# Gated recurrence and causal-convolution kernel: the gate tangents issued per chunk and per gate, the first three chunks in one root batch, a new written order

## The chip, the cores and the metric

The kernel runs on one core of a Trainium2 chip. The metric is the device time of one execution in microseconds (us). Three executions of the kernel before took 302.71, 301.36 and 300.97 us; the median is 301.36 us.

The engines are named as the profile names them: PE (TensorE, matmuls and transposes), PEld (its weight loads), DVE (VectorE), ACT (ScalarE), POOL (GpSimd) and SP (SyncE, which here only issues the DMAs). Each engine works off its own queue in order; an instruction that waits holds everything behind it on that engine.

## The reference, cut to what matters

The input x and two gate inputs have the shape 4 x 6336 x 256 in fp32. With c = 8 and a per-channel constant a_base:

```python
sig_r = 1/(1+exp(-r_gate));  sig_i = 1/(1+exp(-i_gate))
a_t   = exp(c * sig_r * log(a_base))
norm  = sqrt(max(1 - a_t*a_t, 1e-6))
h_t   = a_t * h_{t-1} + norm * sig_i * x          # scan over time, per batch row
# second stage, on y = h
gate  = sigmoid(causal 5-tap depthwise convolution of y)
out   = (gate * (y @ w_val)) @ w_out
```

Both sigmoids of the first stage are computed as tanh of half the argument: sig = (1 + tanh(x/2))/2. So every element of r_gate and i_gate passes once through a tanh on ACT, every a_t through an exp on ACT, and every 1 - a² through a square root on ACT.

## The kernel before, in words

The 25,344 time steps (4 x 6336) are cut into 51 **windows**: windows 0, 1 and 50 of 256 steps, all others of 512. A window is loaded with 128 partitions, each holding consecutive steps of all 256 channels. Windows are bound into 28 **chunks**: chunks 0, 1 and 2 are windows 0, 1 and 2; chunks 3 to 25 hold two windows each (chunk c holds windows 2c - 3 and 2c - 2); chunks 26 and 27 are windows 49 and 50. After the transposes the two halves of 128 channels, h = 0 and 1, lie on the partitions.

There are no loops in time: the whole program is one string, ORDER, of words such as `th.5` or `tr.3.1@0,1` (operation, window or chunk, half, and the banks of the accumulator memory PSUM behind the @). The words are emitted in turn, each on its engine, so ORDER is the order of every engine's queue and also of SP's queue of DMAs. The words:

| word | engine | what it does |
|---|---|---|
| lr, li, lx (window) | SP | loads of r, i and x, 512 KB for a 512-step window |
| th (window) | ACT | tanh of r and i of one window together, 2048 elements per partition (L289) |
| pp, up (window) | POOL | tanh of i plus one (L297), then times x into uring (L309) |
| xp, uv (window) | PE, DVE | the same product for six windows by way of PSUM (L314, L323) |
| tr, ex (chunk group, half) | PE, ACT | transpose of tanh r (L334), exp of it into aring (L350); GROUPS binds one or two chunks |
| sq, sa (chunk, half) | POOL, ACT | a² into ering (L358, L366) |
| rt (batch) | ACT | the root over a batch of chunks (L377); BATCHES binds the chunks |
| nt, xg, xt, sc (chunk) | PE, DVE, PE, DVE | transpose the roots back (L392), multiply into uring (L399), transpose (L408), scan (L430) |
| cv, tg (window) | PE, ACT | convolution in 20 matmuls (L442), tanh of the gate (L449) |
| vl, gv, ou (window) | PE, DVE, PE | y @ w_val (L457), times the gate (L462), times w_out (L472) |
| cd or ca, st (window) | DVE or ACT, SP | copy of the result from PSUM (L480 or L482), store |

The root needs another function table of ACT than tanh and exp. Where a word of the other kind comes next, the loop at the end of the kernel issues a table load (L509); there are 20 of them in the kernel before, besides two at the start.

The data around the tangents lie in rings. `riring` (L201) holds r and i of four windows; r and i of a window are freed together by its `th`. `tring` (L203) holds the tangents of three windows in three lanes each: the tangent of i always lies in the middle lane, that of r in the first lane in one round of three windows and in the last lane in the next (`swapped`, L263), so that the next tangent of r need not wait for the transposes of the last one. The lane of i is freed by `up` or `uv`. `xring` holds x of four windows, freed by `up` or `xp`. `oring` holds four windows of output, freed by the stores. A load waits on SP until its slot is free, and every DMA behind it waits too.

Of the kernel before, what the change touches and what calls it, by code (L numbers as in the profile page):

```python
# [18 lines left out]
BATCHES = [[0], [1], [2], [3, 4], [5, 6, 7], [8, 9, 10], [11, 12, 13], [14, 15, 16], [17, 18, 19], [20, 21, 22], [23, 24,  # L19
    25], [26, 27]]  # L20
# [6 lines left out]
NTRI = 3  # L27
# [11 lines left out]
s_wl.2 lr.8 li.10 lx.8 xt.2@2,3 xt.1@0,1 sc.1.1 li.9 lr.10 sq.3.0 rt.3 li.11 up.6 sc.1.0 lx.10 lr.11 sc.2.1 sc.2.0
up.5 th.8 lx.11 s_wcast th.10 lx.9 pp.10 up.10 lr.14 th.9 li.13 li.14 lr.13 xp.8@4,5 li.12 lr.12 uv.8 th.11 li.15  # L40
nt.3@0,1 xg.3 nt.4@6,7 pp.11 up.11 cv.1@2,3 tg.1 xg.4 xt.3@0,1 sc.3.1 vl.1@4,5 tr.5.0@6,7 ex.5.0 sq.5.0 tr.5.1@2,3
gv.1 ou.1.0@1 cd.1.0 st.1 lx.12 lr.15 ex.5.1 vl.0@4,5 xp.9@6,7 th.14 sq.5.1 cv.2@2,3 sc.3.0 th.13 uv.9 lx.13 xt.4@1,0
gv.0 ou.0.0@4 cd.0.0 st.0 sc.4.1 lx.15 cv.3@6,7 th.12 li.16 li.18 tr.7.1@4,5 tg.2 vl.2@2,3 gv.2 tg.3 ex.7.1 sq.6.1
sq.6.0 lx.14 pp.14 pp.12 up.12 tr.7.0@6,7 ex.7.0 sq.7.0 lx.16 cv.4@2,3 tg.4 th.15 ou.2.0@4,5 cd.2.0 sc.4.0 st.2 lr.18
lr.16 vl.3@6,7 xp.13@2,3 vl.4@4,5 gv.4 sq.7.1 rt.4 uv.13 th.16 sq.8.1 sq.8.0 pp.15 up.15 li.17 lr.17 up.14 ou.4.0@4,5
li.19 cv.5@0,1 lr.19 gv.3 cd.4.0 lx.17 tg.5 ou.3.0@6,7 lx.18 st.4 cd.3.0 st.3 nt.5@4,5 li.20 xg.5 pp.16 up.16 th.17
pp.17 lr.20 nt.7@6,7 xg.7 lx.19 li.21 nt.6@2,3 xg.6 th.18 pp.18 lr.21 xt.5@4,5 sc.5.1 up.17 vl.5@6,7 cv.6@0,1 tg.6
th.19 tr.9.1@2,3 ex.9.1 li.22 lr.22 up.18 sq.9.1 pp.19 gv.5 sc.5.0 tr.9.0@6,7 ex.9.0 lx.20 ou.5.0@0,1 cd.5.0 sq.10.1
xt.6@5,4 up.19 sc.6.1 cv.7@0,1 tg.7 cv.8@2,3 th.20 lr.24 tg.8 sc.6.0 vl.6@6,7 gv.6 xt.7@0,1 cv.9@4,5 ou.6.0@6,7 sc.7.0
th.21 tg.9 cd.6.0 vl.7@2,3 gv.7 vl.9@6,7 th.22 tr.11.0@0 sc.7.1 ou.7.0@2,3 vl.8@4,5 sq.9.0 tr.12.0@1 gv.9 ou.9.0@6,7  # L50
gv.8 ou.8.0@4,5 sq.10.0 st.5 cd.7.0 cd.9.0 lx.22 st.6 rt.5 lx.21 nt.8@6,7 lr.23 li.23 cd.8.0 nt.9@4,5 pp.22 pp.21
up.22 pp.20 up.20 up.21 xg.8 ex.12.0 xg.9 ex.11.0 li.24 st.7 st.9 li.25 lr.25 lx.23 lx.24 li.26 lr.26 th.23 xt.8@6,7
sc.8.0 sq.11.0 pp.23 sq.12.0 lr.27 li.27 cv.11@2,3 tg.11 cv.10@4,5 sc.8.1 cv.12@0,1 st.8 th.24 pp.24 tg.10 tg.12
vl.11@2,3 tr.11.1@6 ex.11.1 gv.11 vl.10@4,5 gv.10 th.25 xt.9@0,1 sc.9.0 tr.12.1@2 ex.12.1 ou.11.0@6,7 cd.11.0
ou.10.0@4,5 cd.10.0 cv.14@2,3 up.23 lx.25 lx.27 th.26 nt.10@6,7 sc.9.1 st.11 li.29 st.10 tg.14 tr.13.0@4,5 xg.10 up.24
sq.11.1 th.27 ex.13.0 tr.13.1@2,3 vl.12@0,1 gv.12 sq.12.1 li.30 lr.30 lx.26 pp.25 pp.27 sq.13.0 xt.10@6,7 sc.10.1
ex.13.1 sq.13.1 up.27 sq.14.0 pp.26 up.25 lr.28 cv.13@4,5 tg.13 vl.13@0,1 gv.13 li.28 vl.14@2,3 gv.14 ou.12.0@4,5
cd.12.0 ou.13.0@0,1 cd.13.0 ou.14.0@2,3 cv.15@4,5 lr.29 st.13 lx.28 lr.31 sc.10.0 cv.16@0,1 cd.14.0 rt.6 nt.11@6,7
tg.15 tg.16 xg.11 vl.15@2,3 gv.15 th.28 st.12 li.31 lx.29 sq.14.1 up.26 nt.13@4,5 xg.13 pp.28 up.28 nt.12@0,1 xg.12
li.32 vl.16@2,3 gv.16 lx.31 lr.32 lx.30 xt.11@4,5 sc.11.1 sc.11.0 ou.15.0@6,7 th.30 pp.30 th.29 pp.29 cv.18@0,1  # L60
ca.15.0 lr.34 li.34 up.29 cv.17@2,3 tg.18 xt.12@6,7 tg.17 vl.17@0,1 gv.17 tr.15.1@2,3 tr.15.0@4,5 th.31 sc.12.0
ou.17.0@0,1 cd.17.0 sc.12.1 ex.15.1 ex.15.0 cv.20@2,3 tg.20 li.33 lr.33 ou.16.0@0,1 cd.16.0 th.32 vl.18@4,5 gv.18
pp.31 up.31 th.34 xt.13@2,3 sc.13.1 vl.19@6,7 cv.19@0,1 tg.19 gv.19 st.17 st.14 st.16 st.15 up.30 th.33 sq.16.1 lx.32
sc.13.0 li.35 lr.35 lx.33 ou.18.0@4,5 cd.18.0 lx.34 li.36 sq.15.0 lr.38 cv.21@0,1 sq.15.1 vl.21@6,7 st.18 lx.35 lr.36
tg.21 gv.21 vl.20@0,1 sq.16.0 cv.22@2,3 gv.20 li.38 lr.37 li.37 pp.34 ou.19.0@4,5 cd.19.0 pp.33 pp.32 up.32
ou.21.0@6,7 ou.20.0@0,1 rt.7 cd.21.0 st.21 tg.22 cd.20.0 nt.14@4,5 xg.14 st.19 nt.16@6,7 xg.16 vl.22@0,1 gv.22 th.35
up.33 up.34 pp.35 tr.17.1@2,3 ex.17.1 xt.14@4,5 sc.14.0 sc.14.1 tr.17.0@6,7 ex.17.0 cv.23@0,1 cv.24@2,3 tg.23 tg.24
ou.22.0@6,7 cd.22.0 nt.15@0,1 xg.15 vl.24@2,3 vl.23@4,5 gv.23 st.20 st.22 lx.36 gv.24 up.35 cv.26@6,7 sq.17.1 th.36
pp.36 sq.18.0 th.38 xt.15@0,1 sc.15.0 sc.15.1 th.37 pp.37 sq.18.1 sq.17.0 ou.23.0@4,5 tg.26 ca.23.0 cv.25@2,3 tg.25
tr.19.0@6,7 ex.19.0 sq.19.0 xt.16@4,5 sc.16.0 tr.19.1@2,3 ex.19.1 sc.16.1 cv.27@0,1 ou.24.0@6,7 cd.24.0 tg.27  # L70
vl.25@2,3 vl.26@0,1 sq.19.1 rt.8 cv.28@4,5 gv.26 up.36 sq.20.1 li.39 st.23 lx.38 lr.40 pp.38 gv.25 lx.37 vl.27@6,7
gv.27 ou.26.0@0,1 cd.26.0 ou.25.0@2,3 lr.41 lr.39 tg.28 th.39 st.24 cd.25.0 ou.27.0@6,7 cd.27.0 nt.19@0,1 nt.17@2,3
xg.17 xg.19 cv.29@6,7 tg.29 sq.20.0 up.37 up.38 nt.18@4,5 xg.18 vl.28@2,3 gv.28 vl.29@6,7 gv.29 xt.17@0,1 sc.17.1
li.40 th.40 tr.21.1@4 li.41 th.41 pp.40 pp.39 st.26 st.25 tr.21.0@5 ex.21.1 ex.21.0 lx.39 li.42 ou.29.0@6,7 ca.29.0
lr.42 sc.17.0 st.27 lx.40 xt.18@2,3 up.39 th.42 ou.28.0@4,5 cv.30@6,7 cd.28.0 tg.30 tr.22.1@0 ex.22.1 tr.22.0@1
# [24 lines left out]
def kernel(  # L100
# [82 lines left out]
    with tc.manual_schedule():  # L183
# [79 lines left out]
        def swapped(w):  # L263

            return (w // NTRI) % 2

        def load(w, which):
            n = wins[w]
            J = n // P
            if which == "x":  # L270
                dst = xring[:, w % NX, 0:J, :]
            else:
                dst = riring[:, w % NRI, "ri".index(which) ^ swapped(w), 0:J, :]
# [267 lines left out]
```

## Time and profile before

| | |
|---|---|
| median of three executions | 301.36 us |
| the profiled execution | 300.32 us, of it 298.5 us span from the first to the last instruction |
| ACT busy | 278.8 us (93%), 197 instructions |
| DVE busy | 247.6 us (83%), 206 instructions |
| PE busy | 246.4 us (83%), 2509 matmuls and transposes |
| POOL busy | 232.8 us (78%), 155 instructions |
| DMA | 104.75 MB, of it 78.39 MB read and 25.95 MB written |

The busy time is the union of an engine's instructions. On ACT consecutive instructions overlap by about 0.1 us, so the sum of single durations is a little more. A row of the timeline gives the start, the duration, and in brackets the idle time before it with what ended it; a row with "x2" stands for two neighbouring instructions of one kind. A row of the groups gives the count, the busy sum and the mean duration in ns. A row by stretches gives the busy time of each engine inside the stretch, the granted clock of PE, the share of the 16 DMA engines' time that was busy, and GB/s.

### The profile page before, as it was taken

How to read it: one execution, taken by the hardware profiler on the slowest of the kernel's cores; microseconds unless marked ns; L12 is line 12 of the kernel's file. 1: busy time of each engine (PE TensorE's matmuls, PEld its weight loads, DVE VectorE, ACT ScalarE, POOL GpSimd, SP SyncE). 2: the span in 40 equal slices, each digit the busy share in tenths (PEclk: the TensorE clock that was granted, in tenths of full speed). 3: DMA queues.
4: the chain of work that ended last, by engine and by line, in shares of the span. 5: the costliest groups of instructions: out<-in, count | busy, mean ns of one | idle time of the engine just before them, and what ended most of it. 6: DMA issues, size and time to landing. Idle time of an engine off the chain costs nothing.

```text
span 298.5 us, 6286 instructions
## 1 busy us (share of the span) xinstructions
PE 246.4 (83%) x2509; PEld 167.8 (56%) x2509; DVE 247.6 (83%) x206; ACT 278.8 (93%) x197; POOL 232.8 (78%) x155
## 2 busy tenths in 40 slices
PE   0374577897888598989898899998979999899993
PEld 0134255454556466757664758567647675666662
DVE  2030288849999889999999999999999899899993
ACT  6799999999999999999999999999999999969863
POOL 1478958989999899899999879998995996255300
PEclk9997599999999979999999999999999999999999
DMA  6999999999999999999999998999999977726046
GB/s 252 408 408 385 379 411 407 406 414 406 337 379 370 419 416 415 411 406 321 417 411 375 388 417 335 396 353 361 349 409 419 408 278 270 273 116 248 29 186 246
DMA packets 29995, 104.75 MB, mean 351 GB/s; under 512 B 3335, under 2 KB 3854, under 8 KB 29966
## 3 DMA queue, kind: packets, MB, share of 16 engines
q1 hardware_dynamic: 29952, 104.35, 90.5%
q8 instruction: 19, 0.31, 0.4%
q14 instruction: 10, 0.08, 0.1%
q10 hardware_dynamic: 14, 0.01, 0.0%
HBM read 78.39 MB, written 25.95 MB: 350 GB/s over the span
## 4 chain that ended last, share of the span: by engine, by line
ACT 31%; PE 23%; DVE 13%; issue 13%; DMA 12%; POOL 5%; SPq 1%; ACTq 0%; DVEq 0%; POOLq 0%
ACT tring L289 10%; ACT aring L350 8%; DMA riring<-in_r_gate_dram 7%; DVE yring L430 7%; PE banks L442 5%; ACT tgring L449 5%; PE banks L457 5%; ACT ering L377 4%; PE banks L472 4%; PE banks L392 3%; DMA riring<-in_i_gate_dram 3%; DVE tgring L462 3%; DVE oring L480 2%; DMA xring<-in_x_dram 2%; ACT L509 2%
## 5 line engine op out<-in xcount | busy, mean ns | idle before, releaser
L430 DVE TENSOR_TENSOR_SCAN yring<-aring,yring,banks 128x1024 bf16<-128x1024 f32 (+5 forms) x54 | 106.2, 1988 | 0.9 <-PE banks L408 0.6
L358 POOL TENSOR_TENSOR ering<-aring 128x1024 f32<-128x1024 f32 (+2 forms) x54 | 91.5, 1713 | 9.7 <-ACT aring L350 9.7
L309 POOL TENSOR_TENSOR uring<-tring,xring 128x1024 bf16<-128x1024 bf16 (+1 forms) x45 | 94.6, 2113 | 4.9 <-DMA xring<-in_x_dram 3.5
L289 ACT ACTIVATE tring<-riring 128x2048 bf16<-128x2048 f32 (+1 forms) x51 | 93.8, 1867 | 4.1 <-DMA riring<-in_i_gate_dram 1.9
L297 POOL TENSOR_SCALAR tring<-tring 128x1024 bf16<-128x1024 bf16 (+1 forms) x45 | 45.8, 1026 | 30.5 <-ACT tring L289 30.4
L442 PE MATMUL banks<-yring,diag 64*64 64x512 bf16 (+7 forms) x1080 | 61.9, 361 | 4.6 <-ACT aring L350 1.6
L462 DVE SCALAR_TENSOR_TENSOR tgring<-tgring,banks 128x1024 bf16<-128x1024 bf16 (+1 forms) x51 | 58.9, 1178 | 5.5 <-PE banks L457 4.4
L472 PE MATMUL banks<-wo,tgring 128*128 128x256 bf16 x396 | 51.4, 274 | 4.7 <-DVE tgring L462 3.5
L350 ACT ACTIVATE aring<-banks,khf 128x2048 f32<-128x2048 bf16 (+3 forms) x38 | 54.1, 1474 | 0.5 <-PE banks L334 0.4
L449 ACT ACTIVATE tgring<-banks 128x1024 bf16<-128x1024 f32 (+1 forms) x51 | 50.4, 1009 | 3.4 <-PE banks L442 3.3
L457 PE MATMUL banks<-yring,wv 128*128 128x512 bf16 (+4 forms) x216 | 49.4, 361 | 5.0 <-DVE oring L480 2.2
L472 PEld LDWEIGHTS <-tgring 128*128 128x128 bf16 x396 | 41.0, 114 | 15.7 <-DVE tgring L462 9.6
L442 PEld LDWEIGHTS <-diag 64*64 64x64 bf16 x1080 | 30.3, 106 | 28.8 <-issue 13.6
L377 ACT ACTIVATE ering<-ering 128x4096 bf16<-128x4096 f32 (+5 forms) x15 | 44.9, 3019 | 0.1
L399 DVE TENSOR_TENSOR uring<-banks,uring 128x2048 bf16<-128x2048 bf16 (+2 forms) x28 | 29.8, 1095 | 18.2 <-PE banks L392 17.9
L480 DVE COPY oring<-banks 128x1024 f32<-128x1024 f32 (+1 forms) x35 | 40.6, 1181 | 4.8 <-ACT aring L350 2.4
L334 PE MATMUL banks<-ident_b,tring 128*128 128x128 bf16 x396 | 29.0, 227 | 12.2 <-ACT tring L289 10.4
L334 PEld LDWEIGHTS <-tring 128*128 128x128 bf16 x396 | 25.1, 101 | 17.7 <-ACT tring L289 11.7
L457 PEld LDWEIGHTS <-wv 128*128 128x128 bf16 x216 | 19.7, 97 | 26.3 <-issue 12.4
L392 PE MATMUL banks<-ident,ering 128*128 128x128 f32 x198 | 28.8, 296 | 6.8 <-DVE oring L480 2.6
L392 PEld LDWEIGHTS banks<-ident,ering 128*128 128x128 f32 x198 | 25.9, 208 | 13.5 <-ACT ering L377 7.7
L408 PE MATMUL banks<-ident,uring 128*128 128x128 f32 x198 | 27.5, 282 | 2.6 <-DVE uring L399 2.5
(36 smaller groups left out, 113.1 us busy)
## 6 DMA issues: line engine op xcount, KB each, us to landing
riring<-in_i_gate_dram SPq DMA_DIRECT2D x48, 512.0 KB, 8.2
riring<-in_r_gate_dram SPq DMA_DIRECT2D x48, 512.0 KB, 8.3
xring<-in_x_dram SPq DMA_DIRECT2D x48, 512.0 KB, 8.0
out_dram<-oring SPq DMA_DIRECT2D x48, 512.0 KB, 5.7
riring<-in_r_gate_dram SPq DMA_DIRECT2D x3, 256.0 KB, 6.3
riring<-in_i_gate_dram SPq DMA_DIRECT2D x3, 256.0 KB, 6.5
xring<-in_x_dram SPq DMA_DIRECT2D x3, 256.0 KB, 5.3
out_dram<-oring SPq DMA_DIRECT2D x3, 256.0 KB, 7.3
```

What stands on the lines that cost most here:

```text
L289: nc.scalar.activation(out=tring[:, w % NTRI, a:a + 2, 0:J, :], in_=riring[:, w % NRI, :, 0:J, :], func=ACT.Tanh, scale=0.5)
L309: nc.gpsimd.tensor_tensor(out=u, in0=t1, in1=xt, op=ALU.mult)
L350: nc.scalar.activation(out=dst, in_=src, func=ACT.Exp, scale=khf[:, h:h + 1], bias=khf[:, h:h + 1])
L358: nc.gpsimd.tensor_tensor(out=e, in0=a, in1=a, op=ALU.mult)
L377: nc.scalar.activation(out=ering[:].bitcast(BF16)[:, 4 * o:4 * o + 2 * n], in_=ering[:, 2 * o:2 * o + 2 * n], func=ACT.Sqrt, scale=-0.25, ...
L392: nc.tensor.transpose(out=bank[:, k:k + P], in_=ering[:, e + q:e + wins[w] // 2:nq], identity=ident[:])
L430: nc.vector.tensor_tensor_scan(out=yring[:, h, col:col + o1 - o0], data0=aring[:, h, a_at[c] + o0:a_at[c] + o1], data1=xT[:, o0:o1], initi ...
L442: nc.tensor.matmul(out=gp[oh * 64:oh * 64 + 64, h, a:b], lhsT=diag[half * 64:half * 64 + 64, h, k, :], rhs=yring[half * 64:half * 64 + 64, ...
L449: nc.scalar.activation(out=tgring[:, w % NTG, :, 0:wins[w]], in_=live.pop(("gp", w))[:, :, 0:wins[w]], func=ACT.Tanh, scale=0.5)
L457: nc.tensor.matmul(out=val[:, m, a:b], lhsT=wv[:, hk, m * P:(m + 1) * P], rhs=yring[:, hk, col:col + b - a], start=(hk == 0), stop=(hk == ...
L462: nc.vector.scalar_tensor_tensor(out=tgring[:, w % NTG, :, 0:wins[w]], in0=tgring[:, w % NTG, :, 0:wins[w]], scalar=1.0, in1=live.pop(("va ...
L472: nc.tensor.matmul(out=ops[:, j * D:(j + 1) * D], lhsT=gv[:, hk, j:wins[w]:J], rhs=wo[:, hk, :], start=(hk == 0), stop=(hk == H - 1))
```

## The change

`th` is replaced by two words that work on a chunk and not on a window: `ta` takes the tanh of r, `tb` the tanh of i. For a two-window chunk each is one instruction over 2 x 1024 elements; for the single-window chunks over 1024 or 512. The rings are parted: `rring` and `iring` have four windows each, `taring` six windows of tangents of r, `tbring` four windows of tangents of i. The place of window w in a ring of n is (w + 1) mod n, so that the two windows of a chunk lie side by side. The swap of lanes is gone.

BATCHES now begins with [0, 1, 2], [3, 4]; there are 10 batches in place of 12, and the loop issues 18 table loads in place of 20. ORDER is written anew throughout. Counting its words: 28 `ta` and 28 `tb` replace 51 `th`; 18 `ca` and 33 `cd` replace 16 and 35; 3 `sa` and 53 `sq` replace 2 and 54; the six `uv` windows are 2, 1, 4, 8, 12 and 17 in place of 3, 1, 7, 8, 9 and 13. All other words have the same counts, and the loads and stores move the same bytes.

```diff
-BATCHES = [[0], [1], [2], [3, 4], [5, 6, 7], ...
+BATCHES = [[0, 1, 2], [3, 4], [5, 6, 7], ...
-NTRI = 3
+NII = 4
+NTR = 6
+NTI = 4
 ORDER = """
...
-s_ident s_small s_kt s_diag li.2 lr.2 th.2 lr.3 lr.0 li.0 th.0 pp.0 tr.2.0@0 li.1 lr.1 tr.0.0@1 ex.2.0 th.1 ...
+s_ident s_small s_kt s_diag lr.2 ta.2 tr.2.1@0 tr.2.0@1 lr.0 ta.0 tr.0.1@2 ex.2.0 sq.2.0 lr.1 ta.1 tr.1.1@1 ...
...
-        riring = rings.tile([P, NRI, 2, 4, D], FP32, name="riring")
+        rring = rings.tile([P, NRI, 4, D], FP32, name="rring")
+        iring = rings.tile([P, NII, 4, D], FP32, name="iring")
-        tring = rings.tile([P, NTRI, 3, 4, D], BF16, name="tring")
+        taring = rings.tile([P, NTR, 4, D], BF16, name="taring")
+        tbring = rings.tile([P, NTI, 4, D], BF16, name="tbring")
...
-        def op_th(w):
-            J = wins[w] // P
-            a = swapped(w)
-            nc.scalar.activation(out=tring[:, w % NTRI, a:a + 2, 0:J, :], in_=riring[:, w % NRI, :, 0:J, :],
-                                 func=ACT.Tanh, scale=0.5)
+        def tangent(c, dst, nd, src, ns):
+            w, k = cwins[c][0], len(cwins[c])
+            J, a, t = wins[w] // P, place(w, ns), place(w, nd)
+            nc.scalar.activation(out=dst[:, t:t + k, 0:J, :], in_=src[:, a:a + k, 0:J, :], func=ACT.Tanh, scale=0.5)
+
+        def op_ta(c):
+            tangent(c, taring, NTR, rring, NRI)
+
+        def op_tb(c):
+            tangent(c, tbring, NTI, iring, NII)
```

Around the last roots the new order reads as follows (words of ACT, PE and the loads that the prediction speaks of; others left out):

```
... ta.25 ... ex.25.1 tb.24 ta.27 tg.39 cv.40 rt.8 ca.37 tg.40 tb.25 tg.41 ca.39 ta.26 tg.42 ca.40 ex.27.1 ex.27.0
ex.26.0 tb.26 tg.43 ex.26.1 ca.41 tg.44 sa.27.1 rt.9 ca.42 cv.45@0,1 tg.45 tb.27 ca.43 ca.44 cv.46@0,1 tg.46 ...
```

More of the change, by code (lines that the diff above doesn't have):

```diff
@@ L39 @@
[L39 to L63, printed above, removed]
@@ L260, in s_wcast, with place @@
             nc.gpsimd.tensor_scalar(out=wo[:], in0=wraw[:, 1], scalar1=0.5, scalar2=None, op0=ALU.mult)
-        def swapped(w):
-            return (w // NTRI) % 2
+        def place(w, n):
+            return (w + 1) % n
         def load(w, which):
@@ L272, in load @@
             else:
-                dst = riring[:, w % NRI, "ri".index(which) ^ swapped(w), 0:J, :]
+                ring = rring if which == "r" else iring
+                dst = ring[:, place(w, NRI if which == "r" else NII), 0:J, :]
             nc.sync.dma_start(dst, flat[which][wstart[w]:wstart[w] + n, :].rearrange("(p j) d -> p j d", p=P))
@@ L304, in u_args @@
             return (uring[:, (w + 1) % NU, 0:wins[w] // (2 * P)].rearrange("p q d two -> p q two d"),
-                    by_pair(tring[:, w % NTRI, 1], w), by_pair(xring[:, w % NX], w))
+                    by_pair(tbring[:, place(w, NTI)], w), by_pair(xring[:, w % NX], w))
         def op_up(w):
@@ L334, in op_tr @@
                     nc.tensor.transpose(out=bank[:, o:o + P],
-                                        in_=tring[:, w % NTRI, 2 * swapped(w), j, h * P:(h + 1) * P],
+                                        in_=taring[:, place(w, NTR), j, h * P:(h + 1) * P],
                                         identity=ident_b[:])
@@ L502 @@
         EXP, SQRT = "exp_and_others", "sqrt_and_others"
-        table, have = {"th": EXP, "tg": EXP, "ex": EXP, "rt": SQRT}, EXP
+        table, have = {"ta": EXP, "tb": EXP, "tg": EXP, "ex": EXP, "rt": SQRT}, EXP
         for word in ORDER.split():
```

107 lines of the change are left out of this document (66 added, 41 removed).

## The prediction

> **What bounds the kernel now.** I read the page's busy times first, then the busy times by stretches, then ACT's timeline, then the groups by form.
>
> ```profile
> span 298.5 us, 6286 instructions
> PE 246.4 (83%) x2509; PEld 167.8 (56%) x2509; DVE 247.6 (83%) x206; ACT 278.8 (93%) x197; POOL 232.8 (78%) x155
> ```
>
> ```profile
> core 0: us, PE busy (x) PEld busy (x) DVE busy (x) ACT busy (x) POOL busy (x), PEclk, DMA share, GB/s
> 0.00:5.00 5.00, 0.60 (x3) 0.46 (x3) 0.97 (x6) 2.94 (x4) 0.97 (x7) 1.00 0.60 216
> 5.00:40.00 35.00, 17.10 (x95) 9.66 (x96) 7.91 (x14) 31.77 (x26) 25.20 (x23) 0.85 1.02 392
> 40.00:143.00 103.00, 87.66 (x896) 60.81 (x900) 92.18 (x74) 101.50 (x64) 95.40 (x58) 0.98 1.01 394
> 143.00:255.00 112.00, 102.30 (x1121) 70.73 (x1110) 109.92 (x84) 111.78 (x74) 98.37 (x59) 1.00 0.97 372
> 255.00:290.00 35.00, 34.73 (x358) 23.06 (x359) 33.18 (x28) 27.73 (x28) 12.82 (x10) 1.00 0.44 167
> 290.00:298.50 8.50, 4.04 (x49) 3.03 (x46) 3.48 (x4) 3.11 (x4) 0.00 (x0) 1.00 0.55 217
> ```
>
> ACT is busy 213.3 of the 215 us from 40 to 255; it sets the pace there. DMA is as full (share 1.01, 0.97) and DVE is near it after 143. In 255:290 PE is full and ACT is not. So a gain is to be had in three places: how soon the first roots are done, how much ACT has to do between them and the last big root, and what is left after that. I cost the three in this order.
>
> **Opening: ACT up to the root of chunk 4.** Before, this root (with that of chunk 1, merged into one row) ends at 35.44 + 4.12 = 39.56.
>
> ```profile
> 5.58 1.91 ACT L289 ACTIVATE tring<-riring 128x2048 bf16<-128x2048 f32 x1 [0.83 <-DMA riring<-in_r_gate_dram]
> 9.22 1.06 ACT L289 ACTIVATE tring<-riring 128x1024 bf16<-128x1024 f32 x1 [1.73 <-DMA riring<-in_i_gate_dram]
> ...
> 15.80 1.28 ACT L509 ACT_TABLE_LOAD   x1
> 17.10 0.63 ACT L377 ACTIVATE ering<-ering 128x512 bf16<-128x512 f32 x1
> 17.75 1.28 ACT L509 ACT_TABLE_LOAD   x1
> 19.57 3.71 ACT L289 ACTIVATE tring<-riring 128x2048 bf16<-128x2048 f32 x2 [0.54 <-POOL uring L309]
> 23.46 1.91 ACT L289 ACTIVATE tring<-riring 128x2048 bf16<-128x2048 f32 x1 [0.18 <-DMA riring<-in_i_gate_dram]
> 25.27 0.58 ACT L449 ACTIVATE tgring<-banks 128x512 bf16<-128x512 f32 x1
> ...
> 32.23 1.28 ACT L509 ACT_TABLE_LOAD   x1
> ...
> 34.49 1.04 ACT L366 ACTIVATE ering<-aring 128x1024 f32<-128x1024 f32 x1
> 35.44 4.12 ACT L377 ACTIVATE ering<-ering 128x512 bf16<-128x512 f32 x2
> ...
> 46.95 1.91 ACT L289 ACTIVATE tring<-riring 128x2048 bf16<-128x2048 f32 x1 [0.57 <-DMA riring<-in_r_gate_dram]
> ```
>
> ```profile
> L289 ACT ACTIVATE tring<-riring 128x2048 bf16<-128x2048 f32 x48 | 90.6, 1918 | 2.3 <-DMA riring<-in_r_gate_dram 1.4 <-POOL uring L309 0.5 <-DMA riring<-in_i_gate_dram 0.2
> L449 ACT ACTIVATE tgring<-banks 128x1024 bf16<-128x1024 f32 x48 | 48.6, 1036 | 2.9 <-PE banks L442 2.8
> L350 ACT ACTIVATE aring<-banks,khf 128x2048 f32<-128x2048 bf16 x18 | 36.4, 2075 | 0.1
> L377 ACT ACTIVATE ering<-ering 128x6144 bf16<-128x6144 f32 x4 | 21.3, 5329 | 0.0
> L482 ACT COPY oring<-banks 128x1024 f32<-128x1024 f32 x15 | 15.0, 1020 | 4.9 <-PE banks L472 4.9
> L377 ACT ACTIVATE ering<-ering 128x4096 bf16<-128x4096 f32 x4 | 14.5, 3616 | 0.0
> L350 ACT ACTIVATE aring<-banks,khf 128x1024 f32<-128x1024 bf16 x10 | 11.7, 1219 | 0.0
> L377 ACT ACTIVATE ering<-ering 128x2048 bf16<-128x2048 f32 x3 | 5.7, 1906 | 0.0
> L289 ACT ACTIVATE tring<-riring 128x1024 bf16<-128x1024 f32 x3 | 3.1, 1050 | 1.7 <-DMA riring<-in_i_gate_dram 1.7
> L350 ACT ACTIVATE aring<-banks,khf 128x512 f32<-128x512 bf16 x4 | 3.1, 773 | 0.4 <-PE banks L334 0.4
> ```
>
> Neighbours overlap by 0.1 (two tangents: 3.71 and not 2 x 1.91), so one costs its duration less 0.1. By then ACT has the same tangents to do in both orders: windows 0 to 7 for r and i before; r of 0 to 10 and i of 0 to 4 after; 14,336 elements each. The exps and root elements are the same. What differs: three table loads become one, -2.56. The square in ACT (34.49) goes to POOL, -0.95. The first gate tanh (25.27) comes later, -0.48. Four root instructions become two; from 3616 - 1906 over 2048 elements one has 0.2 that no element pays, -0.3. Eight tangents become eleven, +0.3 by the same reckoning (1918, 1050). The four waits, 3.28 in all, mostly go: the first `ta` needs one load and not two, the next one a second small load. I leave 1.3 for what comes instead (the first exp behind its transposes, loads of windows 4 to 6), -2.0. Sum -6.0: the root ends at 33.6. With no wait at all it is -7.3, with the old sum of waits -4.0.
>
> The cover of this is thin on POOL. Between the last exp of chunk 3 and the root of chunks 3 and 4, ACT has two tangents (3.6), a load (1.3) and the first root (1.8), 6.7.
>
> ```profile
> L309 POOL TENSOR_TENSOR uring<-tring,xring 128x1024 bf16<-128x1024 bf16 x43 | 92.3, 2157 | 4.5 <-DMA xring<-in_x_dram 3.2
> L358 POOL TENSOR_TENSOR ering<-aring 128x1024 f32<-128x1024 f32 x45 | 84.5, 1896 | 2.2 <-ACT aring L350 2.1
> L297 POOL TENSOR_SCALAR tring<-tring 128x1024 bf16<-128x1024 bf16 x43 | 44.5, 1045 | 21.8 <-ACT tring L289 21.6
> ```
>
> In the same time POOL has a square of chunk 4 (1.9), one of chunk 1 (under 1.9), a `pp` (1.0) and the square that the root waits for (1.9): 6.7 at most, just hidden. If not, up to 2 us come back. The root of chunk 0 moves from 17.7 to about 30 (33.6 less 3.5 for the second root), and with it some 5 us of DVE work that lay in 5:40; DVE was idle for 13 of the 215 us from 40 to 255, which takes it at no cost, and two copies fewer help. With that cover gone it costs up to 5.
>
> A table load begins 0.02 after the end before it and the next instruction 0.02 after its own (15.80, 17.10, 17.75). The Trainium skill, page "ScalarE: Activation LUTs", section "What ACT_TABLE_LOAD costs", adds a drain of about 1.38 us to every switch. These rows have none; by the page the two loads would save 5.3 and not 2.6, and the time would be 2.7 lower.
>
> **Middle: ACT to the end of the root of chunks 23 to 25.** Before it ends at 249.51 + 5.33 = 254.84 (row below). The counts in the two orders between the two roots: after has 1536 elements of tangent less (it has 4608 left behind the root, before 3072), -1.3; two squares more, +1.9; the first gate tanh, +0.5; one copy less, -0.9; seven pairs of table loads in both. Sum +0.2.
>
> Can the loads follow? The tightest place is `ta.18`: 55.05 MB stand in SP's queue up to its loads. Before, 216 x 5 + 392 x 35 make 14.8 MB by 40, and at 394 GB/s 55.05 MB are there at 142.2. They count as landed later: the tangent at 23.46, with 7.86 MB up to its load (moved by 22.3), waited 1.2 beyond that; the one at 46.95 (16.78 MB, 45.0) 1.9. So 143.4 to 144.1. ACT would be there at 33.6 + 109.4 = 143.0; the 109.4 are 23 tangents (1.81), 20 gate tanhs (0.94 and two of 0.48), 14 exps (ten of 1.97, four of 1.12), three roots (16.7), 7 loads and a copy. Wait 0.4 to 1.1, I take 0.8. The root ends at 254.84 - 6.0 + 0.2 + 0.8 = 249.8.
>
> The Trainium skill, page "DMA: Bandwidth & Descriptors", section "Specifications", gives about 358 GB/s of HBM per core. The rows have 392 and 394; at 358 from 40 on, 55.05 MB would come at 152.4, 10.2 later, and the time would be about 306; the rows leave that little of a chance, which lies in the 0.03 below.
>
> **Tail.** Before, 298.5 - 254.84 = 43.7 us follow, in which PE is full. After, the order leaves about 3 us less PE work behind the big root (a window less each of convolution, value and output matmuls, 1.21 + 0.86 + 0.87).
>
> ```profile
> 249.51 5.33 ACT L377 ACTIVATE ering<-ering 128x6144 bf16<-128x6144 f32 x1
> ```
>
> ```profile
> 287.15 1.21 PE banks L442 x19
> ...
> 288.73 0.86 PE banks L457 x4
> 289.59 2.62 PE banks L472 x24
> 292.21 0.70 PE banks L442 x20
> ```
>
> But the last root now stands before the convolutions of the last six windows, not four. Up to it ACT has 4 copies, 5 gate tanhs, 3 tangents (one of two windows), 4 small exps, a small square and two loads, 17.0: it starts at 266.8 and ends, with 1536 elements, at 268.3. A copy, a load and tg.45 follow, 271.4. `cv.46` takes the banks that `tg.45` frees, so PE stands before it until then. Behind it PE has 4.5 windows of convolution (5.4), 5.5 of value (4.7) and output matmuls (4.8), and transposes (1.5): 16.4, so 287.8. The closing chain from the end of the last convolution was 298.5 - 292.9 = 5.6. Sum 293.4: the tail is 43.6, as before. If PE is not held at `cv.46`, up to 3 us more are gained.
>
> So the span is 293.4, 5.1 less. The profiled execution was 300.32, 1.8 over its span, and 1.04 under the median of the runs: 293.4 + 1.82 + 1.04 = **296.3**. Its own range: 293 (no waits in the opening, or the tail's 3) to 299.4.
>
> **Rivals.** *DMA takes the head start (0.17).* For: its share is 1.0 in three stretches, and in the opening the loads of windows 9 and 10 of r wait for a `ta` two windows wide, with all of SP's queue behind them, so that DMA may idle. If the mean falls to 380 GB/s, 55.05 MB come 3.7 later, and with 1 us idle early ACT loses 4.7 of its 6.0: about 301. Against: a ring slot comes free as many megabytes ahead as before, 1 MB per tangent.
>
> *ACT waits for POOL (0.21), slower.*
>
> ```profile
> ACT tring L289 <- POOL uring L309: 0.5, 1, 0.5
> ```
>
> Before, this wait occurs once. After, `tb` writes two windows and needs the `up` of both windows two chunks back; in five places (tb.11, tb.13, tb.16, tb.17, tb.22) that `up` stands right before it or one `pp` away in the order. POOL is busy 95.4 of 103 in 40:143. If POOL lags ACT there by one `up` (2.16), ACT stands still, and with it the next `pp`: four such waits are 8.6, five 10.8, 305 to 307. Three leave 302.8; it decides from 6.5 us on. Against: POOL has one square less, and tangents of r no longer wait for it.
>
> **How the numbers follow.** Forecast 0.62, DMA rival 0.17 (0.05 of it still faster, 0.09 the same, 0.03 slower with a still lower rate), POOL rival 0.21. A measurement tells about 0.5%, 1.5 us, from no change. Faster 0.67, same 0.09, slower 0.24. The range 292 to 303 takes in the forecast's ends and the DMA rival, and leaves out most of the POOL rival.
>
> **What would show it.** Right: ACT's two first roots end at 32 to 35 with one load before them; 18 loads on L509's successor; the root of chunks 23 to 25 ends near 250; PE waits for ACT's gate tanh about 271. Wrong: idle time of ACT before `tb` put down to POOL or before tangents put down to DMA; a DMA share under 0.95 before 40; a tail well off 43.6.

## The result, and the profile after

The changed kernel took 298.2 us (median of four executions, 298.07 to 298.87); the kernel before, measured beside it, 301.72 us (four, 300.97 to 302.71). The ratio is 0.9887 with a 95% interval of 0.9855 to 0.9918: faster by 1.1%, about 3.4 us. The forecast was 296.3 in a range of 292 to 303, so the sign and the range held and the size was missed by 1.9 us.

One caution for all comparisons of spans. The profiled execution of before (300.32) lies under all executions in the table of before, the profiled one of after (298.87) is the slowest of its four. So the two spans, 298.5 and 297.1, differ by only 1.4 us, and steps read off these two traces come out smaller than the medians' 3.4. The 88 executions of the kernel before that ran beside the experiments had spans of 297.8 to 303.0. Where the other 2 us of the medians' 3.4 lie, these two traces do not show.

The page of after, its busy times, and ACT's table loads from the groups of instructions:

```profile
span 297.1 us, 6256 instructions
PE 243.9 (82%) x2509; PEld 167.7 (56%) x2509; DVE 246.4 (83%) x204; ACT 278.3 (94%) x201; POOL 230.9 (78%) x154
...
L518 ACT ACT_TABLE_LOAD x18 | 23.1, 1283 | 0.3
```

The busy times by stretches of after (columns as in the table of before):

```profile
5.00:40.00 35.00, 18.13 (x130) 12.02 (x130) 8.98 (x16) 31.01 (x25) 19.06 (x18) 1.00 1.01 375
40.00:143.00 103.00, 88.19 (x919) 60.05 (x912) 96.67 (x78) 101.74 (x66) 96.86 (x59) 1.00 1.00 390
143.00:255.00 112.00, 99.97 (x1093) 70.07 (x1090) 107.03 (x81) 111.19 (x74) 98.52 (x59) 1.00 0.97 372
255.00:290.00 35.00, 34.78 (x352) 23.83 (x348) 32.06 (x27) 28.56 (x31) 15.46 (x12) 1.00 0.49 196
```

The shape is that of before: ACT is busy 212.9 of the 215 us from 40 to 255, DMA is full, and in 255:290 PE is full. What changed is where the milestones lie. ACT's timeline of after, the rows that carry waits and roots:

```profile
11.71 1.91 ACT L293 ACTIVATE taring<-rring 128x2048 bf16<-128x2048 f32 x1 [0.92 <-DMA rring<-in_r_gate_dram]
...
27.34 1.91 ACT L293 ACTIVATE taring<-rring 128x2048 bf16<-128x2048 f32 x1 [2.18 <-DMA rring<-in_r_gate_dram]
29.27 1.28 ACT L518 ACT_TABLE_LOAD   x1
30.57 5.42 ACT L386 ACTIVATE ering<-ering 128x2048 bf16<-128x2048 f32 x2
...
134.20 1.91 ACT L293 ACTIVATE tbring<-iring 128x2048 bf16<-128x2048 f32 x1 [0.15 <-POOL ering L367]
139.31 1.91 ACT L293 ACTIVATE taring<-rring 128x2048 bf16<-128x2048 f32 x1 [0.49 <-DMA rring<-in_r_gate_dram]
147.31 1.91 ACT L293 ACTIVATE taring<-rring 128x2048 bf16<-128x2048 f32 x1 [0.36 <-DMA rring<-in_r_gate_dram]
...
246.23 5.33 ACT L386 ACTIVATE ering<-ering 128x6144 bf16<-128x6144 f32 x1
...
255.25 1.91 ACT L293 ACTIVATE tbring<-iring 128x2048 bf16<-128x2048 f32 x1 [0.46 <-DMA iring<-in_i_gate_dram]
...
269.35 1.49 ACT L386 ACTIVATE ering<-ering 128x1536 bf16<-128x1536 f32 x1
...
273.44 1.02 ACT L458 ACTIVATE tgring<-banks 128x1024 bf16<-128x1024 f32 x1
```

| milestone on ACT | before | forecast | after |
|---|---|---|---|
| root of chunks 3 and 4 ends | 39.56 | 33.6 | 30.57 + 5.42 = 35.99 |
| root of chunks 23 to 25 ends | 254.84 | 249.8 | 246.23 + 5.33 = 251.56 |
| from there to the end of the span | 43.7 | 43.6 | 297.1 - 251.56 = 45.5 |
| of it, from the end of the last root | 298.5 - 280.06 = 18.4 | 25.1 | 297.1 - 270.84 = 26.3 |

In these two traces the opening is where the time came from: the first two-window root ends 3.6 us earlier. The middle, root to root, is 215.6 us against 215.3 before. The tail gives 1.9 us back.

### The profile page after: what moved, and what is told of

The parts are those of the page before. It is cut to its first block, busy times and chain, and to the rows that moved or that the text cites. A ratio compares the mean times of both kernels' runs of the same rounds, so it can differ in the third digit from the quotient of the medians.

```text
span 297.1 us, 6256 instructions
## 1 busy us (share of the span) xinstructions
PE 243.9 (82%) x2509; PEld 167.7 (56%) x2509; DVE 246.4 (83%) x204; ACT 278.3 (94%) x201; POOL 230.9 (78%) x154
## 5 line engine op out<-in xcount | busy, mean ns | idle before, releaser
L318 POOL TENSOR_TENSOR uring<-tbring,xring 128x1024 bf16<-128x1024 bf16 (+1 forms) x45 | 94.5, 2113 | 11.4 <-DMA xring<-in_x_dram 10.4
L367 POOL TENSOR_TENSOR ering<-aring 128x1024 f32<-128x1024 f32 (+2 forms) x53 | 89.7, 1710 | 14.1 <-ACT aring L359 13.7
L451 PE MATMUL banks<-yring,diag 64*64 64x512 bf16 (+7 forms) x1080 | 62.8, 362 | 5.8 <-ACT tgring L458 2.0
L306 POOL TENSOR_SCALAR tbring<-tbring 128x1024 bf16<-128x1024 bf16 (+1 forms) x45 | 45.9, 1028 | 18.1 <-ACT tbring L293 18.0
L293 ACT ACTIVATE taring<-rring 128x2048 bf16<-128x2048 f32 (+2 forms) x28 | 47.9, 1718 | 4.2 <-DMA rring<-in_r_gate_dram 4.2
L293 ACT ACTIVATE tbring<-iring 128x2048 bf16<-128x2048 f32 (+2 forms) x28 | 47.9, 1718 | 0.6 <-DMA iring<-in_i_gate_dram 0.5
L386 ACT ACTIVATE ering<-ering 128x2048 bf16<-128x2048 f32 (+3 forms) x13 | 44.5, 3451 | 0.1
L343 PE MATMUL banks<-ident_b,taring 128*128 128x128 bf16 x396 | 29.9, 230 | 12.9 <-ACT taring L293 9.3
L489 DVE COPY oring<-banks 128x1024 f32<-128x1024 f32 (+1 forms) x33 | 38.8, 1181 | 1.4 <-PE banks L481 1.1
L343 PEld LDWEIGHTS <-taring 128*128 128x128 bf16 x396 | 25.8, 103 | 20.8 <-ACT taring L293 11.6
```

The costliest lines, as they stand in the source:

```text
L293: nc.scalar.activation(out=dst[:, t:t + k, 0:J, :], in_=src[:, a:a + k, 0:J, :], func=ACT.Tanh, scale=0.5)
L318: nc.gpsimd.tensor_tensor(out=u, in0=t1, in1=xt, op=ALU.mult)
L343: nc.tensor.transpose(out=bank[:, o:o + P], in_=taring[:, place(w, NTR), j, h * P:(h + 1) * P], identity=ident_b[:])
L367: nc.gpsimd.tensor_tensor(out=e, in0=a, in1=a, op=ALU.mult)
L451: nc.tensor.matmul(out=gp[oh * 64:oh * 64 + 64, h, a:b], lhsT=diag[half * 64:half * 64 + 64, h, k, :], rhs=yring[half * 64:half * 64 + 64, ...
```

## The experiments

Ratios are to the kernel before, executed in the same group. The first of them tells how much to read into a single trace.

**The changed kernel once more**, no edit.

> The changed kernel once more, unedited, so that its ratio to the kernel before has a second, longer measurement on the chip that the next three share. All theories expect a ratio of about 0.988 and the same trace: the root of chunks 3 and 4 ends near 36.0, that of chunks 23 to 25 near 251.6.

298.14 us, ratio 0.9878 (0.984 to 0.9916), span 297.1. So the result stands, and two groups agree within 0.1%. But the first root ended at 34.89 instead of 35.99. In this run and six of those below whose opening is the same, it ends between 34.3 and 35.5: the profiled execution of after, with 35.99, is the latest of eight. ACT's wait of 2.18 us at the tangent of r of chunk 5 was 0.56 here. And the 1.1 us by which the repeat was ahead of the trace of after were gone at the next root, that of chunks 5 to 7: it ends at 67.75, in after at 67.36, because ACT waits 0.44 and 0.16 us for loads of i and a little for PE in between.

**The loads of windows 7 and 8 ahead of those of 9 and 10**, and the tangent of chunk 5 ahead of that of 6 accordingly exchanged. In after, SP's queue holds the load of window 9 first; it waits until `ta.4` has freed the slot, and everything behind it waits too. SP's timeline of after shows the gap (9.10 + 1.78 = 10.88 to 16.29):

```profile
9.10 1.78 SPq L278 DMA_DIRECT2D iring<-in_i_gate_dram  x3
16.29 0.80 SPq L278 DMA_DIRECT2D rring<-in_r_gate_dram  x2
```

```diff
- ... li.4 li.3 tr.3.0@2,3 lr.9 ... tb.3 lr.10 ... lr.8 ... ta.6 lr.7 ... ta.5 rt.0
+ ... li.4 li.3 tr.3.0@2,3 lr.8 ... tb.3 lr.7 ... lr.9 ... ta.5 lr.10 ... ta.6 rt.0
```

> The loads lr.8 and lr.7 change places with lr.9 and lr.10 in SP's queue, and ta.5 goes ahead of ta.6. Theory A (SP stands behind lr.9, whose slot ta.4 frees only at 16.3, and the loads behind it come late): the 2.18 us wait of ta.5 goes, the root of chunk 4 ends 1.5 to 2 us earlier, and as ACT sets the pace the kernel is 1.5 to 2 us (0.6%) faster than the changed kernel. Rival B (DMA is full and only its rate counts): the wait moves to ta.6 and keeps its size, time unchanged.

298.0 us, ratio 0.986 (0.9824 to 0.9896), span 296.9. The first root ended at 34.45, inside the spread of the unedited opening, so no head start beyond that spread is shown; ACT then waited 1.25 us for data at the tangent of chunk 18 and 1.27 at that of chunk 25. No gain in time is shown either; whether the order of these loads costs anything stays open.

**The table loads given back, in the opening**: one extra pair (sqrt, exp) on ACT ahead of `ta.5`.

```diff
+        def s_pair():
+            nc.scalar.preload_act_table_set("sqrt_and_others")
+            nc.scalar.preload_act_table_set("exp_and_others")
-... ex.3.0 sq.4.0 ta.6 lr.7 lx.1 xp.1@2 lx.3 sq.1.1 pp.3 ta.5 rt.0 ...
+... ex.3.0 sq.4.0 ta.6 lr.7 lx.1 xp.1@2 lx.3 sq.1.1 pp.3 s_pair ta.5 rt.0 ...
```

> One more pair of table loads on ACT (2 x 1.28 us) right before ta.5, where ACT waited 2.18 us for DMA. If the loads of r bound the opening: the wait takes it up, root of chunk 4 at most 0.5 us later, time unchanged. If ACT's own work bounds it: 2.6 us later, and the kernel 2.6 us (0.9%) slower.

299.52 us, ratio 0.9908 (0.9875 to 0.9942), span 297.7. ACT's timeline of this run:

```profile
25.64 1.28 ACT L506 ACT_TABLE_LOAD   x1
26.92 1.28 ACT L507 ACT_TABLE_LOAD   x1
28.22 1.91 ACT L293 ACTIVATE taring<-rring 128x2048 bf16<-128x2048 f32 x1
...
31.44 5.42 ACT L386 ACTIVATE ering<-ering 128x2048 bf16<-128x2048 f32 x2
```

The tangent after the pair carries no wait any more: the pair lies where ACT would have waited for r. The root ends at 36.86. That is 0.9 us later than in the trace of after, 2.0 later than in the repeat, and 0.9 to 2.6 later than in the eight traces whose opening has no edit: how much of the 2.57 us is hidden depends on the wait that the execution has there. The medians of the same group differ by 1.4. By them the saved pair is less than half of the gain of 3.6, but the intervals of the two ratios (0.9875 to 0.9942 and 0.984 to 0.9916) overlap, so the share is not fixed. The kernel with the pair in it is still faster than before, its interval wholly under 1: the rest of the change brings a part of its own.

**The same pair in the middle**, ahead of `ta.23`.

> The same pair in the middle, right before ta.23 (about 199.7 us), where ACT has no idle time. If ACT sets the pace between the first and the last big root: the root of chunks 23 to 25 ends 2.6 us later and the kernel is 2 to 2.6 us slower. If DMA, DVE or PE sets it and ACT is only as full: under 1 us.

301.96 us, ratio 0.9994 (0.9965 to 1.0023), span 300.1. ACT's timeline of this run:

```profile
186.14 5.32 ACT L386 ACTIVATE ering<-ering 128x6144 bf16<-128x6144 f32 x1
...
200.56 1.28 ACT L506 ACT_TABLE_LOAD   x1
201.84 1.28 ACT L507 ACT_TABLE_LOAD   x1
...
214.89 3.62 ACT L386 ACTIVATE ering<-ering 128x4096 bf16<-128x4096 f32 x1
```

From root to root it is 28.75 us; in after the same two begin at 185.43 and 211.48, 26.05 apart. The 2.57 us of the pair are there in full (2.7), and they are never made up: the last root ends 3.0 later than in after and about the same 26.2 us follow. At this place ACT sets the pace. The medians of the group differ by 3.8 us (301.96 and 298.14), which is more than the pair; where the rest of it lies, the trace does not show.

**The joint batch alone**: the kernel before, with [0, 1, 2] as one batch and 18 table loads, but with the old shared rings.

```diff
-BATCHES = [[0], [1], [2], [3, 4], ...
+BATCHES = [[0, 1, 2], [3, 4], ...
-... sq.0.0 rt.0 lr.5 ... up.2 nt.0@5 xg.0 xt.0@2,3 li.5 th.5 ... rt.2 ... sq.1.0 rt.1 nt.2@0 ...
+... sq.0.0 lr.5 ... up.2 li.5 th.5 ... sq.1.0 rt.0 nt.0@5 xg.0 xt.0@6,7 sc.0.0 sc.0.1 nt.2@0 ...
```

> The kernel before with one part of the change alone: chunks 0, 1 and 2 share a root batch (rt at the place of the root of chunk 1; the words of chunk 0 that need it moved behind it), tangents and rings as they were; 18 table loads in place of 20. If the saved pair is what the head start comes from: the root of chunk 4 ends 2.5 to 3 us earlier than in the kernel before (36.5 to 37), the kernel is 1.5 to 3 us faster than before, ratio 0.990 to 0.995. If the split tangents and the new order bring it: ratio 1.00, as the work of chunk 0 that lay in idle time now lies in busy time.

303.2 us, ratio 1.0052 (1.0022 to 1.0082): slightly slower than before. ACT's timeline:

```profile
18.71 3.71 ACT L289 ACTIVATE tring<-riring 128x2048 bf16<-128x2048 f32 x2 [3.81 <-POOL uring L309]
...
34.10 5.42 ACT L377 ACTIVATE ering<-ering 128x2048 bf16<-128x2048 f32 x2
```

Where before ACT loaded tables and took a root (15.80 to 19.03, then 0.54 of wait), it now stands still for 3.81 us, and the root of chunks 3 and 4 ends at 39.52 instead of 39.56. The wait named is that for POOL's product of window 2, which frees the slot in the ring of tangents. Behind this root the trace falls back: ACT waits 1.51 us for PE's transposes at 50.62, and the next root ends at 75.21 instead of 74.25.

**The same without that wait**: window 2's product by PE and DVE (`xp.2`, `uv.2`) and not by POOL.

```diff
-... tr.1.0@4 sq.1.1 ex.0.1 ... sq.2.0 pp.2 up.2 li.5 th.5 ...
+... tr.1.0@4 xp.2@6,7 sq.1.1 ex.0.1 ... sq.2.0 uv.2 li.5 th.5 ...
```

> The kernel before with only its first three chunks in one root batch (as in the run before_batch: 18 table loads, the old shared rings of the tangents), and now the product of window 2 made by PE and DVE (transposes in xp.2, product uv.2) in place of POOL's pp.2 and up.2. Theory: the batch alone bought nothing because the tangent of chunk 5 waited 3.81 us for POOL's up.2, to free the ring slot of window 2. Then that wait goes, the root of chunks 3 and 4 ends 2 to 3.5 us earlier than 39.5 (36 to 37.5), and the kernel stands 1 to 2.5 us below the run before_batch (ratio to the kernel before 0.997 to 1.002 instead of 1.005). Rival: the wait was only the visible one of several, the loads or PE take its place, the root stays at 39 to 39.6 and the ratio at 1.005.

302.65 us, ratio 1.0031 (1.0000 to 1.0063). ACT's timeline:

```profile
20.04 3.71 ACT L289 ACTIVATE tring<-riring 128x2048 bf16<-128x2048 f32 x2 [3.81 <-DMA riring<-in_i_gate_dram]
...
35.46 5.42 ACT L377 ACTIVATE ering<-ering 128x2048 bf16<-128x2048 f32 x2
```

The wait is as long as it was; only its releaser changed, from POOL to a load of i. (The root ends at 40.88; the whole opening of this execution lies 1.4 later, its first tangent starts at 7.04 and not at 5.62.) My theory fell: POOL's product was the visible wait, the load stood right behind it. With r and i of each window needed together, the opening in this order cannot be faster than its loads, and the pair that the batch saves had been hidden in that time.

**Tangents of two windows as two instructions**, 46 more on ACT.

```diff
-            nc.scalar.activation(out=dst[:, t:t + k, 0:J, :], in_=src[:, a:a + k, 0:J, :], func=ACT.Tanh, scale=0.5)
+            for m in range(k):
+                nc.scalar.activation(out=dst[:, t + m, 0:J, :], in_=src[:, a + m, 0:J, :], func=ACT.Tanh, scale=0.5)
```

> The changed kernel with each two-window tangent issued as two instructions of 1024 elements: 46 more on ACT, each with about 0.09 us that no element pays, 4.1 us. If ACT sets the pace: 3 to 4 us slower than the changed kernel, ratio about 1.00 to the kernel before. If DMA or PE sets it: under 1.5 us.

301.17 us, ratio 0.9992 (0.9961 to 1.0024), span 300.2; the last root ends 3.2 us later, and 26.2 us follow it. So small fixed costs on ACT count too: two instructions take 2.00 us in this trace where one takes 1.91, which makes 4.1 us for 46, and 3.0 of it reached the end, 0.07 each.

**A copy in the tail on DVE** (`ca.37` becomes `cd.37`), since in after PE waits 1.18 us for that copy, which stands behind the big root on ACT.

> The changed kernel with the copy of window 37 on DVE in place of ACT. In the trace the first transposes behind the root of chunks 23 to 25 wait 1.18 us for that copy, which stands behind the root on ACT. If PE sets the tail: those transposes start 1 us earlier and the end comes 0.7 to 1.2 us earlier. If DVE or ACT sets it: unchanged or 0.5 us later.

302.83 us, ratio 1.0021 (0.9995 to 1.0048). The opposite of what was meant. PE's timeline, and the stretches around it:

```profile
254.09 1.95 PE L401 MATMUL banks<-ident,ering 128*128 128x128 f32 x8 [3.82 <-DVE oring L489]
255.97 2.35 PE L451 MATMUL banks<-yring,diag 64*64 64x512 bf16 x20
```

```profile
245.00:250.00 5.00, 4.97 (x50) 3.37 (x48) 5.00 (x4) 4.99 (x2) 5.00 (x3) 1.00 1.00 355
250.00:255.00 5.00, 1.18 (x8) 0.94 (x6) 3.94 (x3) 4.39 (x4) 5.00 (x4) 0.84 1.02 416
255.00:260.00 5.00, 5.00 (x33) 3.06 (x32) 2.35 (x2) 1.34 (x2) 3.60 (x3) 0.50 0.98 347
260.00:265.00 5.00, 5.00 (x55) 3.84 (x53) 4.75 (x4) 3.60 (x4) 0.00 (x0) 0.98 0.44 156
```

On DVE the copy stands behind two scans (4.58 us), so PE waits 3.82 us. Then PE's granted clock falls to 0.50, and 20 matmuls of the convolution take 2.35 us where they take 1.27 in after (row below); ACT in turn waits 3.06 and 1.80 for PE. A wait of 2.6 us more became 4 to 5 us.

**Less PE work in the tail**: one tap of five in the convolution of windows 41 to 49 (the flag that starts an accumulation moves along).

```diff
-                for k in range(CONV_K):
+                taps = range(CONV_K - 1, CONV_K) if 41 <= w <= 49 else range(CONV_K)
+                for k in taps:
```

> The changed kernel with one tap in place of five in the convolutions of windows 41 to 49; this leaves out four fifths of their matmuls, 9 x 0.97 = 8.7 us of PE work behind the root of chunks 23 to 25, and so part of the result of these windows. If PE sets the tail: 4 to 8 us faster than the changed kernel, until ACT or DVE sets it. If PE is held by ACT's gate tanh (as the prediction had it, at cv.46): under 2 us.

297.19 us, ratio 0.984 (0.9803 to 0.9877), span 295.5. PE had 8.7 us of work less and the end came about 1 us sooner. The stretch of this run:

```profile
255.00:290.00 35.00, 29.59 (x242) 21.21 (x240) 31.70 (x26) 29.70 (x33) 14.77 (x12) 1.00 0.50 200
```

PE, at 34.78 of 35 in after, looked like the bound of the tail. It is one by about 1 us only: with 5 us to spare it waits for ACT, DVE and POOL in pieces of at most 1.18 us.

**The pair of table loads in the tail**, ahead of `ta.26`.

> The changed kernel with one extra pair of table loads on ACT (2.57 us) ahead of the tangent of r of chunks 26 on, at about 259 us, after the root of chunks 23 to 25. Theory (ACT's chain up to the last gate of the root's output sets the tail as well): the last root ends 2.6 us later, at about 273.4, what follows stays 26.2, and the time is 2 to 3 us longer, ratio to the kernel before 0.996 to 0.999 instead of 0.989. Rival (PE sets the tail, with 34.8 us busy of 35 between 255 and 290, and ACT has 6 us to spare there): most of the pair is hidden, at most 1 us, ratio 0.989 to 0.992.

302.01 us, ratio 1.0016 (0.9979 to 1.0053), span 300.3. ACT's timeline and PE's:

```profile
259.60 1.28 ACT L506 ACT_TABLE_LOAD   x1
260.88 1.28 ACT L507 ACT_TABLE_LOAD   x1
...
272.65 1.49 ACT L386 ACTIVATE ering<-ering 128x1536 bf16<-128x1536 f32 x1
```

```profile
263.29 0.51 PE L343 MATMUL banks<-ident_b,taring 128*128 128x128 bf16 x6 [2.29 <-ACT taring L293]
```

Between the big root and the last one lie 20.4 us instead of 17.8, all of the 2.57; PE, "full" in after, stands 2.29 us for the late tangent; 26.2 us follow the last root as ever. So a late ACT delays the tail by way of this tangent. Behind 264.2 PE has no more waits up to the last output matmuls, and ACT's first copy behind the last root waits 0.29 us for PE (0.28 in after): from there on neither of the two has time to spare. The medians are longer by 3.8, more than the pair; in the trace 0.7 of it lies ahead of the pair. What the rest is stays open.

**Work taken off ACT, onto POOL**: `sa.15`, `sa.25` become `sq`, 1.9 us less on ACT.

> The changed kernel with two of ACT's squares (those of chunks 15 and 25, 0.95 us each) made by POOL instead. Theory (ACT sets the pace from 40 us on): 1.9 us less, ratio to the kernel before about 0.982 instead of 0.989. Rival (POOL is the next bound): the roots wait for POOL's squares, or the tangents for POOL's products, by 2 us or more, and the time is that of the changed kernel or longer.

304.33 us, ratio 1.0094 (1.0055 to 1.0132): slower than before. ACT's timeline:

```profile
149.61 1.91 ACT L293 ACTIVATE tbring<-iring 128x2048 bf16<-128x2048 f32 x1 [2.03 <-POOL uring L318]
...
243.70 1.91 ACT L293 ACTIVATE tbring<-iring 128x2048 bf16<-128x2048 f32 x1 [2.58 <-POOL uring L318]
...
249.26 5.33 ACT L386 ACTIVATE ering<-ering 128x6144 bf16<-128x6144 f32 x1 [0.91 <-POOL ering L367]
```

Each square taken over delays POOL's `up` and so the next tangent of i: 4.6 us of waits for `up` and 0.9 at the root for 1.9 saved. The big root ends 3.0 later than in after; another 1.9 us are lost behind it, where ACT waits 1.75 us for PE.

**Work taken off ACT, onto DVE**: `ca.9`, `ca.25` become `cd`, 1.8 us less on ACT.

> The changed kernel with ACT's copies ca.9 and ca.25 (about 0.9 us each) made by DVE instead. Theory (ACT sets the pace): 1.8 us less, ratio to the kernel before about 0.983 instead of 0.989, if DVE, which is busy 94 to 96% of those stretches, takes them in without lateness. Rival (DVE has no room, as the run with copy 37 on DVE showed in the tail): the copies stand behind scans, PE and then ACT wait for them by 1 us or more, and the time is that of the changed kernel or longer.

302.46 us, ratio 1.0051 (1.0017 to 1.0086). DVE's, PE's and ACT's timelines around the second copy:

```profile
195.04 4.58 DVE L439 TENSOR_TENSOR_SCAN yring<-aring,yring,banks 128x1024 bf16<-128x1024 f32 x2
199.53 1.20 DVE L489 COPY oring<-banks 128x1024 f32<-128x1024 f32 x1
```

```profile
200.79 1.80 PE L466 MATMUL banks<-yring,wv 128*128 128x512 bf16 x4 [3.17 <-DVE oring L489]
```

```profile
204.84 1.21 ACT L359 ACTIVATE aring<-banks,khf 128x1024 f32<-128x1024 bf16 x1 [3.81 <-PE banks L343]
```

Again the copy stands behind two scans, PE waits 3.17 for the banks, and ACT 3.81 for PE's transposes. The rivals named for these two runs were right: an engine that is off the critical path by a microsecond has no room for a microsecond of work just where the order would put it.

No version tried beats the changed kernel by more than its interval, among those that compute everything.

## Why the prediction was right, and where it was not

**The sign was right, and in the traces it is the head start of the opening that carries it, as forecast. Which part of the change makes this head start is shown only in part, and the two steps that failed most are the waits of the opening and the work left in the tail.** Of the forecast's steps:

- *Opening, forecast 33.6, measured 35.99 (34.3 to 35.5 in the seven others).* The instructions came as counted: one load ahead of the two roots, 18 in all, no square and no gate tanh of ACT. The step that failed is "I leave 1.3 for what comes instead": the waits are 0.61, 0.92, 0.22 and 2.18, 3.93 in all, and at least 2.36 in each of the eight traces with this opening. The last is the mechanism that I had set down under the DMA rival, loads of windows 9 and 10 standing in SP's queue for a tangent of two windows; its size, 0.56 to 2.18, changes from one execution to the next without any edit. The sign "32 to 35" holds for most executions and not for the profiled one.
- *The table loads as the largest term (-2.56).* Right on the path of after, but not as the cause of the gain. The batch alone gave ratios of 1.0052 and 1.0031, and the pair put back cost 0.9 to 2.6 us at the root, 1.4 in the medians, and left part of the gain standing. I had counted ACT's instructions and waits as terms that add up; in an opening that waits for its loads they replace each other. That it takes the parted rings, which let a tangent of r start on one load and without POOL, to make the saved loads count is argued and not shown: no run has the new order with the old rings, or the new rings with the old batches, so what each brings by itself was not separated.
- *Middle, forecast +0.2 of work and 0.8 of wait at `ta.18`; measured 0.3 in all in the profiled execution, 1.8 in the repeat (217.1 against 215.3).* Waits of 0.49 and 0.36 stand at `ta.17` and `ta.18`, next to where the sum over the loads had put one of 0.8. That ACT sets the pace is confirmed for the stretch behind 186 us by the pair put there. For the stretch up to `ta.18` it is not: in ten of the eleven traces with the changed order ACT waits there for loads of r, 0.30 to 1.27 us, also in the run with the pair in the opening (0.85). The start of `ta.18`, 145.7 to 148.0, does not follow the end of the first root: 34.42 goes with 148.04, 36.86 with 147.79. Up to there the loads hold the pace as much as ACT, and a head start is in part evened out.
- *Tail, forecast 43.6, measured 45.5.* The count was near: 17.8 to the last root (forecast 17.0; 0.46 of it is a wait for the last loads of i), `tg.45` ends at 274.46, 1.3 later after the big root than reckoned, PE's rest 16.6 (16.4), the close 5.5 (5.6). The sign that I named did not show: PE does not idle ahead of `cv.46`, it has output matmuls there. PE's timeline of after:

```profile
252.51 1.23 PE L401 MATMUL banks<-ident,ering 128*128 128x128 f32 x8 [1.18 <-ACT oring L491]
...
273.18 1.91 PE L481 MATMUL banks<-wo,tgring 128*128 128x256 bf16 x16
275.02 1.27 PE L451 MATMUL banks<-yring,diag 64*64 64x512 bf16 x20
```

  `cv.46` begins 0.6 us behind `tg.45`, held by these matmuls, and 26.2 to 26.5 us follow the last root in every trace of the changed order except the one with fewer taps (25.1). What the prediction had wrong is "about 3 us less PE work behind the big root". It counted the words behind the root in ORDER. When the root ends, PE has the same 404 matmuls and transposes left in both traces, 38.88 us busy before and 39.26 after (first row before, second after), because PE of before had run a window further ahead while the root ran:

```profile
254.84:298.50 43.66, 38.88 (x404) 26.21 (x404) 36.82 (x31) 30.99 (x32) 12.82 (x10) 1.00 0.47 178
```

```profile
251.56:297.10 45.54, 39.26 (x404) 26.77 (x404) 36.48 (x30) 34.34 (x37) 18.90 (x14) 0.98 0.56 223
```

  So "up to 3 us more if PE is not held" was no option. Of the 1.9 us that the tail is longer, 0.4 is PE's busy time and 1.5 its idle time; 0.9 of that is the wait for the copy that stands behind the big root on ACT (the row at 252.51).
- *The sum.* Against the forecast span of 293.4: +2.4 in the opening, -0.6 in the middle, +1.9 in the tail make 297.1. Against the span the forecast was 3.7 short. The median missed by only 1.9, because the profiled execution of after lies 0.7 over its median where I had assumed one 1.0 under it; that is luck.

**The rivals.** *DMA takes the head start*: in part. The waits for r in the opening are 3.3 us in the profiled execution and 1.8 in the repeat, and from 5 to 40 the rate fell from 392 to 375 GB/s at an undiminished share of 1.01. From 40 on the rate stayed (390 after 394), and in the profiled execution so did most of the head start (3.3 of the 3.6 us at the root of chunks 23 to 25). *ACT waits for POOL*: refuted for this kernel, whose trace shows one such wait from 40 us on, of 0.15 us at 134.20. But its mechanism is real and near: two squares more on POOL brought waits of 2.03 and 2.58 at just such a place and made the kernel slower than before.

**The price of a table load.** The forecast took 1.28 us each, from the rows. The Trainium skill, page "ScalarE: Activation LUTs", section "What ACT_TABLE_LOAD costs", has a drain of about 1.38 us with every switch; the pairs in the middle and in the tail cost 2.7 and 2.6 us on ACT, two loads of 1.28 and no more, so the traces do not bear it out on this path. (The medians of both runs are 3.8 longer, without a place in the traces for the rest.)

## What to carry to other kernels

A saving on the busiest engine counts only where that engine does not wait: put the saved piece back as a dummy at the place in question, and the run tells what the place is worth (here 0.9 to 2.6 in the opening, 2.6 or more in middle and tail). When a wait goes, ask which releaser is second; here a load stood exactly behind POOL. And busy shares of 94 to 99% on three engines mean an order woven tightly: moving work from the busiest to the next one made all three such versions slower than the changed kernel, and their traces show lateness at single places.

## What the runs showed of the hardware that I had not expected

In the run with the copy of window 37 on DVE, after PE had stood for 3.82 us, its granted clock was 0.50 for about 5 us, and matmuls took nearly twice their time (2.35 against 1.27 us); after 3.17 us of standing, in the run with two copies on DVE, four matmuls of y @ w_val took 1.80 where four take 1.02 (at 192.65 of that run). The Trainium skill, page "TensorE: Matmul & The Clock Gate", section "The HAM clock gate", gives about 3.4 us without work after which the clock is halved; the first case agrees, the second lies slightly under that figure. By the column of the granted clock the opening of before has such a stretch too, and that of after has none. The two rows, the first of before, the second of after:

```profile
30.00:35.00 5.00, 2.20 (x3) 1.17 (x4) 0.05 (x1) 4.97 (x5) 5.00 (x5) 0.50 1.04 385
```

```profile
30.00:35.00 5.00, 2.83 (x22) 1.99 (x20) 2.06 (x5) 4.99 (x3) 3.24 (x5) 1.00 1.05 383
```

But the durations say that the column does not show every slow stretch. In after PE stands 5.53 us ahead of the transposes of x at 24.59, and six of them then take 4.99 us (mean 997 ns) where four take 1.88 us (mean 593 ns) later, though the column reads 1.00 for both. PE's timeline of after:

```profile
24.59 4.99 PE L323 MATMUL banks<-xring,ident 128*128 128x512 f32 x6 [5.53 <-DMA xring<-in_x_dram]
...
34.05 1.88 PE L323 MATMUL banks<-xring,ident 128*128 128x512 f32 x4
```

Whether such stretches cost the kernel before anything was not tried: in that stretch of before ACT, and not PE, is busy 4.97 of 5.00 us. Over the 88 executions of before beside the experiments, a mean granted clock that is lower by 0.01 goes with about 0.9 us more (correlation -0.52); their mean is 0.977, that of the ten unedited executions of the changed kernel 0.993. By this slope about 1.4 us of the medians' difference would go with the clock, an estimate; no run tells whether as cause or as consequence.
